# Attention and token-mixing MLP on one core: the fourth term of VectorE's exponential tiles by an accumulating DMA

## The chip, the cores and the metric

The kernel runs on one core of a Trainium2 chip. The metric is the device time of one execution in microseconds. The median of three runs of the kernel before is 754.1 us (753.49 to 754.58). All work is on one core: TensorE (PE) multiplies, ScalarE (ACT) and VectorE (DVE) compute elementwise, GpSimd (POOL) does little, SyncE (SP) issues the DMAs.

## What is computed

The input x has 2048 tokens of 640 features. It is normalised, goes through attention with 32 heads of 20 features, and is gated by a token-mixing MLP.

```python
xn = _layernorm(x, axis=-1)
# attention: 32 heads of 20
scores = einsum("bhqd,bhkd->bhqk", q, k) * (Dh ** -0.5)
p = softmax(scores, axis=-1)
o = einsum("bhqk,bhkd->bhqd", p, v)
s = o.reshape(B, S, D) @ wo
# MLP over the tokens, F = 1536
u = gelu(einsum("bsd,sf->bdf", layernorm(xn), w1) + b1)
g = silu(einsum("bdf,fs->bds", u, w2) + b2)
return x + s * g
```

What matters here is the softmax: 32 x 2048 x 2048 exponentials.

## The kernel before, in words

**Units and passes.** Scores are computed transposed: keys on the 128 partitions, queries along the free axis. A *unit* is one block of 128 keys by 512 queries of one head. Heads are taken in eight groups of four; a *pass* is one group with 512 queries, so 16 key blocks by 4 heads, 64 units. There are 2048 units in all. The four heads of a group are row-tiled on TensorE (32 rows each), so up to four score matmuls run side by side (`emit_st`, L1283). Values are column-tiled, four heads side by side (`emit_pv`, `pv_mm`, L1381), and accumulate in one PSUM bank.

**Two ways to the exponential.** ScalarE takes units in groups of two or three PSUM banks and writes exact exponentials as bf16 into `pt_sb` (`emit_exp`, L1313). VectorE takes *quads*, the four heads of one key block. For each head it adds a constant to the scaled score, clamps it at zero and rounds it to uint16 (`emit_op1`, L1324); the bits of this integer, read as bf16, are a piecewise linear approximation of the exponential. The result goes to buffer 0 of the quad in `dt_sb`, 128 x 4 x 512. To make the approximation better, the integer is shifted by the constants `DK = (0, 32, 64, 96)`: three more buffers of the quad get buffer 0 plus 32, 64 and 96 (`emit_top`, L1362, one instruction of 128 x 2048 each). The sum of the four, weighted by `AK`, is the exponential. The weights sit in the values: term 0 is multiplied with `v_sb`, terms 1 to 3 with scaled copies `vs_sb`. So a quad costs TensorE four value bursts, one for each term, where four units of ScalarE cost one.

**Who takes what.** Only the five key blocks in `RC` of each pass may become quads, since only for these are scaled values kept. `d_claimable` gives one out if a buffer is free, fewer than `NLIVE` quads are live and 16 units of the pass are left, else from the next pass. VectorE's units get a PSUM bank in two ways: the last bank of a three-bank group is lent to VectorE (`do_st`, if `dve_load` is below `LEND`), or the spare bank `JB` is used.

**Order of the work.** The order of the instructions on each engine is fixed when the program is built. The class `Prog` keeps a time for each engine; the main loop of `schedule` asks `pe_cands` and `eng_cands` what each engine could do next, takes what can start first by priority, and adds its planned cost. Hardware semaphores then hold each instruction until what it needs is done, but an engine never goes past its first waiting instruction. Besides scores and values, TensorE gets the projections, the MLP and the output product as *jobs* with priorities and due times (`add_job`, `add_bank_job`). `row_piece` puts single row-tiled steps of an MLP job beside scores that leave a row group free. `emit_fill` (L1398) adds zero products where TensorE would stand still. All DMAs are issued from SP on eight semaphore lanes (`Prog.dma`).

**Buffers.** `dt_sb` has `NTILE` = 8 buffers. A quad takes one at its first unit and one for each further term; a buffer comes free once the value product of its term is planned, buffer 0 once all terms are written and its own product is planned. `dquads` holds the quads whose values are due; only the first of the current pass is looked at.

Of the kernel before, what the change touches and what calls it, by code (L numbers as in the profile page):

```python
# [10 lines left out]
P = 128  # L11
# [28 lines left out]
class Prog:  # L40
# [3 lines left out]
    COMPUTE = ("pe", "act", "dve", "pool", "sp")  # L44
    LAT = {"pe": 55.0, "act": 55.0, "dve": 55.0, "pool": 80.0, "sp": 60.0}
    TAIL = {"pe": 170.0, "act": 118.0, "dve": 82.0, "pool": 60.0, "sp": 0.0}

    def __init__(self, nc, n_lanes=8):
        self.nc = nc
        self.n_lanes = n_lanes  # L50
        self.cengs = list(self.COMPUTE) + [f"d{i}" for i in range(n_lanes)]
# [8 lines left out]
        self.pipe = 0.0  # L60
        self.pe_end = 0.0
        self.low = 0
        self.lowt = 0.0
        self.alog = []
# [21 lines left out]
    def _add(self, eng, ceng, fn, reads, writes, name, extra_req=(), cost=100.0, tail=None):  # L86
# [50 lines left out]
        t.t0 = start  # L137
        if ceng not in self.COMPUTE:
            start = max(start, 700.0)
            if tail is not None:  # L140
                self.T[eng] = start + cost
                self.pipe = max(self.pipe, start) + cost
                t.fin = self.pipe - cost + tail
            else:
                self.T[eng] = start + 450.0
                self.pipe = max(self.pipe, start + 600.0) + cost
                t.fin = self.pipe + (1200.0 if self.pipe < 2500.0 else 2800.0 if cost > 800.0 else 1400.0)
        else:
            self.T[eng] = start + cost
            self.busy[eng] += cost  # L150
            t.fin = start + cost + (self.TAIL[eng] if tail is None else tail)
# [32 lines left out]
    def dma(self, fn, reads=(), writes=(), name="dma", lane=None, cost=3000.0, over=(), tail=None):  # L184
# [12 lines left out]
        return t  # L197

    def final_waits(self):
        for li in range(self.n_lanes):  # L200
# [10 lines left out]
    def emit(self, sems):  # L211
# [12 lines left out]
        def make(engname):  # L224
            def body(eng):
                for t in self.tasks[engname]:
# [5 lines left out]
                    ins = t.fn(eng)  # L232
                    if engname == "sp" and t.ceng.startswith("d"):
# [32 lines left out]
class _Kern:  # L266
# [9 lines left out]
    JB = 7  # L276
    RC = (0, 3, 6, 9, 12)
    NT = 2
# [6 lines left out]
    QK_LEAD = 6.0  # L285
    SLACK, MINJ = 0.0, 640.0
    ROOM = 6
    ROWM, ROWP, ROWN = 5, 2, 400
    lastrow = None
    MERGE = False  # L290
    OPM = 2
# [15 lines left out]
    SHARE = True  # L307
    VPRIO = 25.0
    QAT = (0.0, 0.0, 0.0, 0.0)
    ACTP = 30.0  # L310
    COLS = True
    NTILE, NLIVE, EARLY = 8, 3, True
    QC = ((0.5, 3.0), (3.2, 6.4), (9.0, 13.5), (14.0, 18.0), (19.0, 22.0))
# [4 lines left out]
    OPTS = (  # L318
        ("SLACK", (120.0, 40.0, 200.0, 320.0)),
        ("MINJ", (640.0, 320.0, 1000.0)),  # L320
        ("ROOM", (3, 6, 0)),
        ("DRIDE", (400.0, 150.0, 700.0)),
        ("LEND", (1800.0, 1300.0, 2400.0, 700.0, 0.0)),
        ("PARTS", ((2,), (2, 1), (3, 1), (1,), ())),
        ("LATE", (2.0, -9.0, 99.0)),
        ("DON", (True, False)),
        ("LONE", (False, True)),
        ("CONFL", (True, False)),
        ("TOPP", (38.0, 22.0)),
        ("EVP", (24.0, 36.0)),  # L330
        ("FGAP", (40.0, 150.0)),
        ("GROT", (1, 0)),
    )
    PLAN = ()
# [18 lines left out]
    def build(self):  # L353
# [4 lines left out]
        with es:  # L358
# [18 lines left out]
            sb("pt_sb", [P, self.RP, 512], bf)  # L377
            sb("dt_sb", [P, self.NTILE, 4, 512], u16)
            sb("zt_sb", [P, 2, 2, self.D], bf)
            sb("tr_sb", [P, 512], f32)  # L380
# [18 lines left out]
            for i in range(pr.n_lanes):  # L399
                sems[f"d{i}"] = E(nc.semaphore(f"sem_d{i}"))  # L400
            self.t = t
            self.schedule()
# [8 lines left out]
    def schedule(self):  # L411
# [716 lines left out]
        dquads = []  # L1128
        tfree = list(range(self.NTILE))
        dlive = [0]  # L1130
        dop1 = []
# [68 lines left out]
        def d_claimable():  # L1200
            if not self.DON:
                return None
            if tfree and dlive[0] < self.NLIVE:
                q0 = a_cur[0]
# [36 lines left out]
        def d_take(g, bk):  # L1241
            d = d_cur[0]
            if d is None:
                q, c, r = d_claimable()
                claimed.add((q, c))
                dlive[0] += 1
                d = d_cur[0] = dict(q=q, c=c, r=r, todo=[0, 1, 2, 3], tl=[tfree.pop(0), None, None, None], fin=[0.0] * 4, left=4, pk=0)
                stats["dve_units"] += 4
                nd_pass[q] += 1
# [70 lines left out]
        def emit_op1():  # L1320
# [12 lines left out]
            if d["left"] == 0:  # L1333
                dtop.append([d, 1])
                d["fin"][0] = tk.fin
                if self.EARLY:
                    dquads.append((0.0, d))

        def emit_top():
            d, k = dtop[0]  # L1340
# [26 lines left out]
            for j in range(k, k + n):  # L1367
                d["fin"][j] = tk.fin
            if k + n == 4:
                dtop.pop(0)  # L1370
                if not self.EARLY:
                    dquads.append((tk.fin, d))
                for j in range(2 if n == 2 else 1):
# [38 lines left out]
        def emit_pv(items, quads):  # L1412
# [4 lines left out]
            ends = [d for d, n_ in quads if d["pk"] + n_ == 4]  # L1417
            freed = []
            for d, n_ in quads:
                for k in range(d["pk"], d["pk"] + n_):  # L1420
                    for g in range(4):
                        seq.append(("d", d, k, g))
                    if k > (1 if self.MERGE else 0) or d["tl"][3] is not None:
                        freed.append(d["tl"][k])
                d["pk"] += n_
            items = sorted(items, key=lambda x: (x[3], x[1][2]))
            for x in items:
# [12 lines left out]
            for i, s in enumerate(seq):  # L1440
# [15 lines left out]
                else:  # L1456
# [8 lines left out]
                    avail.remove((fin, u, s0))  # L1465
            tfree.extend(freed)
            for d in ends:
                dlive[0] -= 1
                dquads[:] = [x for x in dquads if x[1] is not d]
# [83 lines left out]
        for w in (1, 0):  # L1553
# [3 lines left out]
        rw.append(("tag", "wr"))  # L1557
        add_job("wr", rw, ("xTd15",), 30.0)
        add_job("bload", [
            ("dma", small(lambda e: e.dma_start(bload_sb[:, 0:FC], B_b1.rearrange("(fc p) -> p fc", p=P))), [], [S_("bl1")],  # L1560
# [216 lines left out]
        def pe_cands(T):  # L1777
# [28 lines left out]
            if acc_ok[0] and pv_pass[0] < NP:  # L1806
# [5 lines left out]
                    f"v{half}_{y[0]}" in done and f"vs{G}_{r}" in done for y, r in zip(units[q][x[1]["c"]], x[1]["r"]))]  # L1812
                quads = quads[:1]
                pick, cnt = [], [0] * 4
# [20 lines left out]
                okp = bool(pick) and (min(cnt) >= 1 or len(pick) == rem or (tail and len(mine)))  # L1835
                if quads:
                    d0 = quads[0][1]
                    have = sum(f > 0.0 for f in d0["fin"])
                    left = have - d0["pk"]
                    whole = have == 4  # L1840
                    if left > 0 and whole:
                        if min(cnt) >= 1 or rem == len(pick):
                            pv.append(mk(pick, [(quads[0], left)]))
                            if len(pick) < rem or not pick:
                                pv.append(mk([], [(quads[0], left)]))
                        else:
                            pv.append(mk([], [(quads[0], left)]))
                    for n in self.PARTS:
                        if n < left or (n == left and not whole):
                            pv.append(mk([], [(quads[0], n)]))  # L1850
                if okp:
# [4 lines left out]
            for j in active:  # L1856
                s = j.steps[j.i]
                if s[0] == "pe":
                    late = late or now - j.at > self.LATE
                    n = 0  # L1860
                    for z in j.steps[j.i:]:
                        if z[0] == "row":
                            continue
                        if z[0] != "pe":
                            break
                        n += z[5]
                    jb.append((j.prio, pr.ready("pe", s[2], s[3]), lambda j=j: do_step(j, "pe"), s[5], n,
                               "pv" if len(s) > 6 else "full"))
            if ramp[0] or nomore_a():
                c = [x[:3] for x in ([sta] if sta else []) + ([std] if std else []) + pv + jb]  # L1870
# [74 lines left out]
        def dve_load(T):  # L1945
            x = max(0.0, pr.T["dve"] - T) + 602.0 * len(dop1)
            for d, k in dtop:
                x += (1730.0 if k == 1 else 1130.0) if self.MERGE else 600.0 * (4 - k)
            return x

        def row_piece(used):
# [48 lines left out]
        def do_st(grp, us):  # L2000
            T = pr.T["pe"]
            lend = None
            if (len(grp) >= self.LEND_MIN and len(us) == len(grp) and dveready[0] and (not ramp[0] or self.RLEND)
                    and dve_load(T) < self.LEND):
                lend = d_pick({u[2] for u in us[:-1]})
# [76 lines left out]
        def loads():  # L2082
# [8 lines left out]
            for x in {id(x): x for x in live}.values():  # L2091
                pe += 216.0 * (4 - x["pk"])
                d += (1730.0 if x["fin"][1] == 0.0 else 1130.0 if x["fin"][3] == 0.0 else 0.0) if self.MERGE else (
                    597.0 * sum(f == 0.0 for f in x["fin"][1:]))
            return a - done_cost["act"], pe - done_cost["pe"], d - done_cost["dve"]
# [5 lines left out]
        while True:  # L2101
# [17 lines left out]
            if (nomore or (a_cur[0] == NP - 1 and a_left(NP - 1) < self.D_GUARD)) and d_cur[0] is None and not dop1:  # L2119
                if not bankq and JB not in busybanks and JB not in bank_off:  # L2120
                    bank_off.add(JB)
# [15 lines left out]
            if bt is None:  # L2137
                break
            r, e = bt
# [46 lines left out]
```

## Time and profile before

| What | Value | How to read it |
|---|---|---|
| median of three runs | 754.1 us | 753.49 to 754.58 |
| profiled execution | 754.1 us | its own time |
| span of its profile | 752.3 us | first to last instruction; 1.8 us lie around it |
| granted TensorE clock | 0.999 | mean over the span |
| value products of quads, L1381 | 1536 + 512 matmuls | terms 1 to 3 with `vs_sb`, term 0 with `v_sb` |
| value products of ScalarE's units | 1616 matmuls | from `pt_sb` |
| score matmuls, L1283 | 2128, 376 ns mean | up to four side by side |
| GpSimd, 60 to 730 us | 0.6 us busy | one memset |
| DMA | 42.66 MB, mean 57 GB/s | all from SP, bursts for the MLP's weights |

Columns of a group line are: line, engine, operation, output<-input, shapes, count, then busy us, mean ns of one, and the engine's idle time just before them with what ended it. A matmul's end is modelled and neighbours overlap, so TensorE's busy time isn't TensorE at its peak; distances from start to start tell more.

### The profile page before, as it was taken

How to read it: one execution, taken by the hardware profiler on the slowest of the kernel's cores; microseconds unless marked ns; L12 is line 12 of the kernel's file. 1: busy time of each engine (PE TensorE's matmuls, PEld its weight loads, DVE VectorE, ACT ScalarE, POOL GpSimd, SP SyncE). 2: the span in 40 equal slices, each digit the busy share in tenths (PEclk: the TensorE clock that was granted, in tenths of full speed). 3: DMA queues.
4: the chain of work that ended last, by engine and by line, in shares of the span. 5: the costliest groups of instructions: out<-in, count | busy, mean ns of one | idle time of the engine just before them, and what ended most of it. 6: DMA issues, size and time to landing. Idle time of an engine off the chain costs nothing.

```text
span 752.3 us, 23672 instructions
## 1 busy us (share of the span) xinstructions
PE 716.3 (95%) x10561; PEld 243.6 (32%) x10561; DVE 719.0 (96%) x1320; ACT 730.0 (97%) x707; POOL 15.3 (2%) x23
## 2 busy tenths in 40 slices
PE   9899999999999999999999999999999999999997
PEld 7332222222233232323223332323233332333233
DVE  7889999999999999999999999999999999999996
ACT  5989999999999999999999999999999999999995
POOL 4200000000000000000000000000000000000000
PEclk9999999999999999999999999999999999999999
DMA  8754111110121031212111131301325501041102
GB/s 237 155 110 48 56 38 37 20 38 5 38 62 20 13 76 31 72 24 69 20 38 21 30 87 24 74 13 29 79 76 81 128 28 51 7 152 47 47 15 70
DMA packets 119738, 42.66 MB, mean 57 GB/s; under 512 B 79172, under 2 KB 118468, under 8 KB 119588
## 3 DMA queue, kind: packets, MB, share of 16 engines
q1 hardware_dynamic: 119636, 41.15, 23.4%
q8 instruction: 82, 1.34, 0.8%
q14 instruction: 20, 0.16, 0.1%
HBM read 26.37 MB, written 10.22 MB: 49 GB/s over the span
## 4 chain that ended last, share of the span: by engine, by line
ACT 76%; PE 18%; DVE 6%; issue 0%; DVEq 0%
ACT pt_sb L1313 74%; PE ps_all L1381 5%; PE ps_all L1283 5%; PE ps_all L648 5%; DVE dt_sb L1324 1%; PE ps_all L1408 1%; ACT zt_sb L849 1%; DVE dt_sb L1362 1%; ACT zt_sb L844 1%; DVE bst_sb L532 1%; DVE bst_sb L530 1%; DVE regC L548 1%; PE ps_all L965 1%; PE ps_all L633 0%; DVE v_sb L1114 0%; PE ps_all L746 0%
## 5 line engine op out<-in xcount | busy, mean ns | idle before, releaser
L1313 ACT ACTIVATE pt_sb<-ps_all 128x1024 bf16<-128x1024 f32 (+1 forms) x681 | 711.2, 1242 | 4.9 <-PE ps_all L1283 2.1
L1324 DVE TENSOR_SCALAR dt_sb<-ps_all 128x512 uint16<-128x512 f32 x496 | 328.4, 683 | 15.9 <-PE ps_all L1283 8.9
L1283 PE MATMUL ps_all<-qk_sb 32*128 32x512 bf16 (+1 forms) x2128 | 269.1, 376 | 26.4 <-ACT pt_sb L1313 22.9
L1362 DVE TENSOR_SCALAR dt_sb<-dt_sb 128x2048 uint16<-128x2048 uint16 x372 | 241.2, 689 | 1.5
L1283 PEld LDWEIGHTS ps_all<-qk_sb 32*128 32x128 bf16 x2128 | 68.4, 91 | 280.9 <-ACT pt_sb L1313 226.4
L1381 PE MATMUL ps_all<-dt_sb,vs_sb 128*21 128x512 bf16 (+1 forms) x1536 | 130.7, 376 | 0.9 <-DVE dt_sb L1362 0.5
L1381 PE MATMUL ps_all<-pt_sb,v_sb 128*21 128x512 bf16 (+1 forms) x1616 | 127.0, 374 | 1.9 <-DVE v_sb L1114 0.9
L648 PE MATMUL ps_all<-regC,regA 128*32 128x128 bf16 (+1 forms) x1472 | 65.5, 297 | 0.0
L648 PE MATMUL ps_all<-regB,regA 128*32 128x128 bf16 (+1 forms) x1480 | 65.2, 298 | 0.3 <-DVE qs_sb L698 0.3
L1381 PEld LDWEIGHTS ps_all<-dt_sb,vs_sb 128*21 128x21 bf16 x1536 | 33.4, 90 | 51.7 <-issue 31.2
L1381 PE MATMUL ps_all<-dt_sb,v_sb 128*21 128x512 bf16 (+1 forms) x512 | 49.2, 377 | 0.1
L1381 PEld LDWEIGHTS ps_all<-pt_sb,v_sb 128*21 128x21 bf16 x1616 | 30.9, 90 | 49.2 <-issue 35.9
L648 PE MATMUL ps_all<-xnT_sb,wqk_sb 128*32 128x512 bf16 x640 | 46.1, 382 | 0.0
L648 PEld LDWEIGHTS ps_all<-regB,regA 128*32 128x32 bf16 x1480 | 27.4, 96 | 23.3 <-issue 10.9
L648 PEld LDWEIGHTS ps_all<-regC,regA 128*32 128x32 bf16 x1472 | 27.8, 96 | 22.0 <-issue 10.6
L965 PE MATMUL ps_all<-wv_sb,xnT_sb 128*128 128x512 bf16 (+1 forms) x160 | 27.3, 301 | 0.0
L656 PE MATMUL ps_all<-regC,regA 32*128 32x512 bf16 x64 | 24.6, 384 | 0.0
L648 PE MATMUL ps_all<-wv_sb,xnT_sb 128*32 128x480 bf16 x320 | 22.1, 369 | 0.3 <-DVE qs_sb L1117 0.3
L1505 DVE STREAM_TRANSPOSE tr_sb<-ps_all 128x512 f32<-128x512 f32 x31 | 22.0, 711 | 0.0
L656 PE MATMUL ps_all<-regB,regA 32*128 32x512 bf16 x56 | 21.5, 384 | 0.0
L1381 PEld LDWEIGHTS ps_all<-dt_sb,v_sb 128*21 128x21 bf16 x512 | 13.0, 90 | 20.6 <-issue 14.2
L1398 PE MATMUL ps_all<-wp_sb,zw_sb 128*21 128x512 bf16 (+1 forms) x244 | 19.4, 373 | 0.0
(88 smaller groups left out, 348.5 us busy)
## 6 DMA issues: line engine op xcount, KB each, us to landing
regA<-in_B_w_dram SPq DMA_DIRECT2D x6, 1024.0 KB
regA<-in_B_w_dram SPq DMA_DIRECT2D x8, 768.0 KB
qk_sb<-qk_scratch_dram SPq DMA_DIRECT2D x56, 80.0 KB
qk_scratch_dram<-qs_sb SPq DMA_DIRECT2D x32, 128.0 KB
regA<-in_A_x_dram SPq DMA_DIRECT2D x6, 640.0 KB
ok_scratch_dram<-on_sb SPq DMA_DIRECT2D x96, 20.0 KB
out_dram<-regC SPq DMA_DIRECT2D x3, 640.0 KB
wqk_sb<-in_A_wqkv_dram SPq DMA_DIRECT2D x2, 480.0 KB
```

Of the source, the lines that this page charges most:

```text
L530: steps.append(("dve", lambda e, b=b: e.bn_stats(bst_sb[:, b, 0:6], regA[:, b, 0:320]), [sx], [s0], f"{nm}s0", 393.0))
L532: steps.append(("dve", lambda e, b=b: e.bn_stats(bst_sb[:, b, 6:12], regA[:, b, 320:640]), [sx], [s1], f"{nm}s1", 393.0))
L648: fns.append(lambda e, c=c, e_=e_: e.matmul(oc(c, e_), lhsT[:, c:e_], rhs, start=start, stop=stop, tile_position=(0, c)))
L656: row = lambda g: (lambda e: e.matmul(oc(0, 128), lhsT[32 * g:32 * g + 32, :], rhs[32 * g:32 * g + 32, :], start=False, stop=False, tile_p ...
L965: steps.append(("pe", lambda e, c=c: e.matmul(ap, oT_sb[:, c, b * 128:(b + 1) * 128], wo_ap[:, c, c0:c0 + n], start=(opens and c == 0), st ...
L1283: t = pr.pe(lambda e, outp=outp, lhsT=lhsT, rhs=rhs, g=g: e.matmul(outp, lhsT, rhs, start=True, stop=True, tile_position=(32 * g, 0)), rea ...
L1313: tk = pr.act(lambda e: e.activation(outp, inp, AF.Exp, scale=math.log(2.0) / 128.0), reads=[bank_slot[b] for b in banks[:n]], writes=[S_( ...
L1324: tk = pr.dve(lambda e: e.tensor_scalar(w, src, WOFF, 0.0, ALU.add, ALU.max), reads=[bank_slot[bk]], writes=[S_(f"dt{d['tl'][0]}_{g}")], n ...
L1362: tk = pr.dve(lambda e: e.tensor_scalar(dst, src, dk, None, ALU.add), reads=[S_(f"dt{b}_{g}") for b in inb for g in range(4)], writes=[S_( ...
L1381: pr.pe(lambda e: e.matmul(outp, lhsT, rhs, start=(k == 0), stop=last, tile_position=(0, 32 * g)), reads=reads, writes=[bank_slot[AB]], na ...
L1398: pr.pe(lambda e, outp=outp, rhs=rhs, g=g: e.matmul(outp, zw_sb[:, 0:DH + 1], rhs, start=False, stop=False, tile_position=(0, 32 * g)), re ...
L1505: steps.append(("dve", lambda e: e.transpose(tr_sb[:, :], ps(AB)), [bank_slot[AB]], [S_("tr")], f"epT{q}", 632.0))
```

## The change

For most quads the third L1362 (the fourth term, plus 96) is replaced by one DMA. A new tile `kc_sb`, 128 x 4 x 512 of uint16, is filled once with 96 by GpSimd. Once the value product of term 0 is planned, `emit_x` issues from GpSimd a DMA that adds `kc_sb` to buffer 0 in place, 512 KB; buffer 0 then holds the fourth term. So such a quad needs three buffers, not four. `x_ok` says which quads qualify: the planned queue of these transfers is at most 4 us behind VectorE's planned time, and the quad's pass isn't ScalarE's current one or has at least 16 units left. Other quads do the fourth term on VectorE as before.

The planner gets four lanes for these transfers and three costs: 950 ns on GpSimd to issue, 2900 ns to move, 2700 ns to land. The list of quads whose values are due may go past quads that lack only their fourth term. `dve_load` and the planned loads count the work left out. Besides:

- `NTILE` 8 to 7 (one buffer's room goes to `kc_sb`), `NLIVE` 3 to 4
- `RC` from (0, 3, 6, 9, 12) to (2, 5, 8, 11, 14)
- `SLACK` 0 to 80: scores for ScalarE may be planned 80 ns later than its need
- `ROWP` 2 to 1; `row_rest` now finishes row-tiled steps that are left over, at the end of a job or when nothing else can run
- `VPRIO` 25 to 24.5, `ACTP` 30 to 22
- the bank `JB` is given to the tail only once all MLP products are planned

`OPTS`, `LENDH`, `LEND1`, `JLATE` and `DLAG` change nothing as they stand: `PLAN` is empty in both, and the limits aren't reached.

```diff
+    NXL = 4
+    XISSUE, XMOVE, XTAIL = 950.0, 2900.0, 2700.0
...
+        if eng == "pool" and ceng != "pool":
+            self.T[eng] = start + self.XISSUE
+            self.xpipe = max(self.xpipe, start + self.XISSUE) + self.XMOVE
+            t.fin = self.xpipe + self.XTAIL
...
-    RC = (0, 3, 6, 9, 12)
+    RC = (2, 5, 8, 11, 14)
...
-    SLACK, MINJ = 0.0, 640.0
+    SLACK, MINJ = 80.0, 640.0
...
-    NTILE, NLIVE, EARLY = 8, 3, True
+    NTILE, NLIVE, EARLY = 7, 4, True
+    XLEFT, XQ = 16, 4000.0
...
+        def x_ok(d):
+            if "kc" not in done or pr.xpipe > pr.T["dve"] + self.XQ:
+                return False
+            return d["q"] > a_cur[0] or a_left(d["q"]) >= self.XLEFT
+
+        def emit_x(d):
+            b0 = d["tl"][0]
+            dst = dt_sb[:, b0, :, :]
+            sl_ = [S_(f"dt{b0}_{g}") for g in range(4)]
+            t = pr.xdma(lambda e: e.dma_start(dst, kc_sb[:, :, :], accum_op=ALU.add), [S_("kc")] + sl_, sl_,
+                        f"dX{d['q']}_{d['c']}")
+            d["tl"][3] = b0
+            d["fin"][3] = t.fin
...
-            if k + n == 4:
+            if k == 2 and not self.MERGE and x_ok(d):
+                d["x"] = True
                 dtop.pop(0)
...
+                if d["pk"] >= 1:
+                    emit_x(d)
+            elif k + n == 4:
+                dtop.pop(0)
...
+                if d["x"] and d["pk"] < 4 and d["tl"][3] is None:
+                    xs.append(d)
...
             tfree.extend(freed)
+            for d in xs:
+                emit_x(d)
...
+        add_job("kc", [("pool", lambda e: e.memset(kc_sb[:, :, :], int(self.DK[3])), [], [S_("kc")], "kc", 1800.0), ("tag", "kc")],
+                ("lnp14",), 43.0)
...
-                quads = quads[:1]
+                k = 0
+                while k < len(quads) - 1 and quads[k][1]["x"] and quads[k][1]["pk"] == 3:
+                    k += 1
+                quads = quads[:k + 1]
```

More of the change, by code (lines that the diff above doesn't have):

```diff
@@ L50, in __init__ @@
         self.n_lanes = n_lanes
-        self.cengs = list(self.COMPUTE) + [f"d{i}" for i in range(n_lanes)]
+        self.cengs = list(self.COMPUTE) + [f"d{i}" for i in range(n_lanes)] + [f"x{i}" for i in range(self.NXL)]
         self.cidx_of = {c: i for i, c in enumerate(self.cengs)}
@@ L60, in __init__ @@
         self.pipe = 0.0
+        self.xpipe = 0.0
+        self.xn = 0
         self.pe_end = 0.0
@@ L137, in _add @@
         t.t0 = start
-        if ceng not in self.COMPUTE:
+        if eng == "pool" and ceng != "pool":
+            self.T[eng] = start + self.XISSUE
+            self.xpipe = max(self.xpipe, start + self.XISSUE) + self.XMOVE
+            t.fin = self.xpipe + self.XTAIL
+        elif ceng not in self.COMPUTE:
             start = max(start, 700.0)
@@ L197, in dma, with xdma @@
         return t
+    def xdma(self, fn, reads, writes, name):
+        ceng = f"x{self.xn % self.NXL}"
+        self.xn += 1
+        t = self._add("pool", ceng, fn, reads, writes, name, extra_req=self.ctasks[ceng][-1:])
+        t.need_inc = True
+        return t
     def final_waits(self):
@@ L232, in body @@
                     ins = t.fn(eng)
-                    if engname == "sp" and t.ceng.startswith("d"):
+                    if t.ceng not in self.COMPUTE:
                         ins.then_inc(sems[t.ceng], 16)
@@ L285 @@
     QK_LEAD = 6.0
-    SLACK, MINJ = 0.0, 640.0
+    SLACK, MINJ = 80.0, 640.0
     ROOM = 6
-    ROWM, ROWP, ROWN = 5, 2, 400
+    ROWM, ROWP, ROWN = 5, 1, 400
     lastrow = None
+    LENDH, LEND1, JLATE = 0.0, 9999.0, 0.0
     MERGE = False
@@ L307 @@
     SHARE = True
-    VPRIO = 25.0
+    VPRIO = 24.5
     QAT = (0.0, 0.0, 0.0, 0.0)
-    ACTP = 30.0
+    ACTP = 22.0
     COLS = True
-    NTILE, NLIVE, EARLY = 8, 3, True
+    NTILE, NLIVE, EARLY = 7, 4, True
+    DLAG = 99.0
+    XLEFT, XQ = 16, 4000.0
     QC = ((0.5, 3.0), (3.2, 6.4), (9.0, 13.5), (14.0, 18.0), (19.0, 22.0))
@@ L318 @@
     OPTS = (
-        ("SLACK", (120.0, 40.0, 200.0, 320.0)),
+        ("SLACK", (0.0, 120.0, 40.0, 200.0, 320.0)),
         ("MINJ", (640.0, 320.0, 1000.0)),
-        ("ROOM", (3, 6, 0)),
+        ("ROOM", (6, 3, 0)),
         ("DRIDE", (400.0, 150.0, 700.0)),
         ("LEND", (1800.0, 1300.0, 2400.0, 700.0, 0.0)),
-        ("PARTS", ((2,), (2, 1), (3, 1), (1,), ())),
-        ("LATE", (2.0, -9.0, 99.0)),
+        ("PARTS", ((3, 1), (2,), (2, 1), (1,), ())),
+        ("LATE", (1.0, 2.0, -9.0, 99.0)),
         ("DON", (True, False)),
@@ L329 @@
         ("TOPP", (38.0, 22.0)),
-        ("EVP", (24.0, 36.0)),
-        ("FGAP", (40.0, 150.0)),
+        ("EVP", (36.0, 24.0)),
+        ("FGAP", (0.0, 40.0, 150.0)),
         ("GROT", (1, 0)),
+        ("JOBF", (4, 0, 8)),
     )
@@ L378, in build @@
             sb("dt_sb", [P, self.NTILE, 4, 512], u16)
+            sb("kc_sb", [P, 4, 512], u16)
             sb("zt_sb", [P, 2, 2, self.D], bf)
@@ L400, in build @@
                 sems[f"d{i}"] = E(nc.semaphore(f"sem_d{i}"))
+            for i in range(pr.NXL):
+                sems[f"x{i}"] = E(nc.semaphore(f"sem_x{i}"))
             self.t = t
@@ L1129, in schedule @@
         tfree = list(range(self.NTILE))
+        kc_sb = t["kc_sb"]
         dlive = [0]
@@ L1202, in d_claimable @@
                 return None
+            if bankq and not ramp[0] and nclaim[0] / UP - bankq[0].at > self.DLAG:
+                return None
             if tfree and dlive[0] < self.NLIVE:
@@ L1246, in d_take @@
                 dlive[0] += 1
-                d = d_cur[0] = dict(q=q, c=c, r=r, todo=[0, 1, 2, 3], tl=[tfree.pop(0), None, None, None], fin=[0.0] * 4, left=4, pk=0)
+                d = d_cur[0] = dict(q=q, c=c, r=r, todo=[0, 1, 2, 3], tl=[tfree.pop(0), None, None, None], fin=[0.0] * 4, left=4, pk=0, x=None)
                 stats["dve_units"] += 4
@@ L1337, in emit_op1 @@
                     dquads.append((0.0, d))
+        def x_ok(d):
[10 more added lines that the diff above has]
+            d["fin"][3] = t.fin
+            stats["x"] = stats.get("x", 0) + 1
         def emit_top():
@@ L1368, in emit_top @@
                 d["fin"][j] = tk.fin
-            if k + n == 4:
+            if k == 2 and not self.MERGE and x_ok(d):
+                d["x"] = True
                 dtop.pop(0)
-                if not self.EARLY:
-                    dquads.append((tk.fin, d))
+                if d["pk"] >= 1:
+                    emit_x(d)
+            elif k + n == 4:
+                dtop.pop(0)
                 for j in range(2 if n == 2 else 1):
@@ L1417, in emit_pv @@
             ends = [d for d, n_ in quads if d["pk"] + n_ == 4]
-            freed = []
+            freed, xs = [], []
             for d, n_ in quads:
@@ L1835, in pe_cands @@
                 okp = bool(pick) and (min(cnt) >= 1 or len(pick) == rem or (tail and len(mine)))
-                if quads:
-                    d0 = quads[0][1]
-                    have = sum(f > 0.0 for f in d0["fin"])
+                for qd in quads:
+                    d0 = qd[1]
+                    have = next((i for i, f in enumerate(d0["fin"]) if f == 0.0), 4)
                     left = have - d0["pk"]
@@ L1842, in pe_cands @@
                         if min(cnt) >= 1 or rem == len(pick):
-                            pv.append(mk(pick, [(quads[0], left)]))
+                            pv.append(mk(pick, [(qd, left)]))
                             if len(pick) < rem or not pick:
-                                pv.append(mk([], [(quads[0], left)]))
+                                pv.append(mk([], [(qd, left)]))
                         else:
-                            pv.append(mk([], [(quads[0], left)]))
+                            pv.append(mk([], [(qd, left)]))
+                    elif left > 0 and d0["x"] and left not in self.PARTS:
+                        pv.append(mk([], [(qd, left)]))
                     for n in self.PARTS:
                         if n < left or (n == left and not whole):
-                            pv.append(mk([], [(quads[0], n)]))
+                            pv.append(mk([], [(qd, n)]))
                 if okp:
@@ L1868, in pe_cands @@
                                "pv" if len(s) > 6 else "full"))
+                elif s[0] == "row" and nclaim[0] == NALL:
+                    x = j.rowstep[j.i]
+                    jb.append((j.prio, pr.ready("pe", x[2], x[3]), lambda j=j: row_rest(j), 320.0, 320.0, "st"))
             if ramp[0] or nomore_a():
@@ L1947, in dve_load, with row_rest, lend_ok @@
             for d, k in dtop:
-                x += (1730.0 if k == 1 else 1130.0) if self.MERGE else 600.0 * (4 - k)
+                x += (1730.0 if k == 1 else 1130.0) if self.MERGE else 600.0 * ((3 if x_ok(d) else 4) - k)
             return x
+        def row_rest(j):
+            x = j.rowstep[j.i]
+            for g in sorted(j.rows[j.i]):
+                self.lastrow = pr.pe(x[7](g), reads=x[2], writes=x[3], name=x[4] + "r", cost=pe_cost("st", 320.0), w=53.0,
+                                     after=self.lastrow)
+            j.rows[j.i].clear()
+            settle(j)
+        def lend_ok(T):
+            if max(0.0, pr.T["dve"] - T) + 602.0 * len(dop1) >= self.LEND1:
+                return False
+            x = dve_load(T)
+            if x < self.LEND:
+                return True
+            if x >= self.LENDH or not bankq:
+                return False
+            return nclaim[0] / UP - bankq[0].at < self.JLATE
         def row_piece(used):
@@ L2003, in do_st @@
             if (len(grp) >= self.LEND_MIN and len(us) == len(grp) and dveready[0] and (not ramp[0] or self.RLEND)
-                    and dve_load(T) < self.LEND):
+                    and lend_ok(T)):
                 lend = d_pick({u[2] for u in us[:-1]})
@@ L2093, in loads @@
                 d += (1730.0 if x["fin"][1] == 0.0 else 1130.0 if x["fin"][3] == 0.0 else 0.0) if self.MERGE else (
-                    597.0 * sum(f == 0.0 for f in x["fin"][1:]))
+                    597.0 * sum(f == 0.0 for f in x["fin"][1:3 if x["x"] else 4]))
             return a - done_cost["act"], pe - done_cost["pe"], d - done_cost["dve"]
@@ L2119, in schedule @@
             if (nomore or (a_cur[0] == NP - 1 and a_left(NP - 1) < self.D_GUARD)) and d_cur[0] is None and not dop1:
-                if not bankq and JB not in busybanks and JB not in bank_off:
+                if not bankq and JB not in busybanks and JB not in bank_off and all(x in done for x in m2pe):
                     bank_off.add(JB)
@@ L2137, in schedule @@
             if bt is None:
-                break
+                j = next((j for j in active if j.steps[j.i][0] == "row"), None)
+                if j is None:
+                    break
+                row_rest(j)
+                continue
             r, e = bt
```

## The prediction

> **What bounds the kernel now.** I read the page's busy times first, then one stretch of the table by stage (40 us, after the ramp, to 740 us, before the tail), then the groups by form, the waits, and last a few lines of the timeline. Columns of the stage line: start:end, length, then busy us and instruction count of PE, PEld, DVE, ACT and POOL.
>
> ```profile
> PE 716.3 (95%) x10561; PEld 243.6 (32%) x10561; DVE 719.0 (96%) x1320; ACT 730.0 (97%) x707; POOL 15.3 (2%) x23
> ...
> 40.00:740.00 700.00, 672.31 (x10090) 217.24 (x10090) 680.09 (x1188) 698.53 (x677) 0.63 (x1) 1.00 0.21 48
> ...
> ACT 76%; PE 18%; DVE 6%; issue 0%; DVEq 0%
> ```
>
> Between 40 and 740 us ScalarE is idle for 1.5 us of 700, VectorE for 20, TensorE for 28. The chain of waits is ScalarE's exponentials for three quarters. So ScalarE sets the end, VectorE is the second owner of the same work (the exponentials of 2048 score units), and TensorE, which serves both, is nearly full.
>
> ```profile
> L1313 ACT ACTIVATE pt_sb<-ps_all 128x1024 bf16<-128x1024 f32 x491 | 481.3, 1127 | 0.9 <-PE ps_all L1283 0.5
> L1324 DVE TENSOR_SCALAR dt_sb<-ps_all 128x512 uint16<-128x512 f32 x496 | 328.4, 683 | 15.9 <-PE ps_all L1283 8.9 <-PE ps_all L656 5.7
> L1313 ACT ACTIVATE pt_sb<-ps_all 128x1536 bf16<-128x1536 f32 x190 | 285.9, 1541 | 4.0 <-PE ps_all L1381 1.9 <-PE ps_all L1283 1.7
> L1362 DVE TENSOR_SCALAR dt_sb<-dt_sb 128x2048 uint16<-128x2048 uint16 x372 | 241.2, 689 | 1.5
> L1398 PE MATMUL ps_all<-wp_sb,zw_sb 128*21 128x512 bf16 x224 | 18.5, 382 | 0.0
> ```
>
> Here the reader sees the split: 496 units, 124 quads of four, are VectorE's, the other 1552 ScalarE's. A quad costs VectorE 4 x 328.4/496 + 3 x 241.2/372 = 2.65 + 1.94 = 4.59 us; everything else on VectorE is 719.0 - 328.4 - 241.2 = 149.4 us. A unit taken from ScalarE turns a 1536-wide exponential into a 1024-wide one: 1541 - 1127 = 414 ns, so 1.66 us a quad. L1398 is filler: 61 bursts of four with the 20 narrow ones, put where TensorE would stand still.
>
> ```profile
> 301.17 0.39 PE L1283 MATMUL ps_all<-qk_sb 32*128 32x512 bf16 x3
> ...
> 301.50 0.40 PE L1381 MATMUL ps_all<-dt_sb,v_sb 128*21 128x512 bf16 x4
> ...
> 301.72 0.39 PE L648 MATMUL ps_all<-regC,regA 128*32 128x512 bf16 x4
> ...
> 302.04 0.39 PE L1283 MATMUL ps_all<-qk_sb 32*128 32x512 bf16 x3
> ```
>
> Four column-tiled matmuls start 0.22 us before the next four (301.50 to 301.72); between row-tiled and column-tiled ones lie 0.32 or 0.33, so a switch costs 0.10 to 0.11. TensorE runs back to back here.
>
> **What the Trainium skill says.** "DMA: Bandwidth & Descriptors", section "SWDGE vs HWDGE vs iDMA": an accumulating DMA can only be issued from GpSimd, whose cores write its descriptors. Its section "Anatomy of one DMA" gives about 2.0 us plus bytes/436e3 us for one. "Collectives: The Full Stack", section "The bandwidth ceiling", says that an adding transfer reads two sources and so runs at half rate. The trace of before has no accumulating DMA and cannot confirm these. "SBUF — State Buffer", section "Who interferes with whom": GpSimd and a VectorE instruction that uses both ports exclude each other for a whole instruction. With this the trace agrees, in the one place of the middle where GpSimd works:
>
> ```profile
> 518.78 0.63 POOL L1669 MEMSET wqk_sb<- 128x640 bf16 x1 [485.07 <-PE ps_all L691]
> ...
> 518.94 1.62 DVE L1362 TENSOR_SCALAR dt_sb<-dt_sb 128x2048 uint16<-128x2048 uint16 x2
> ```
>
> Two L1362 take 1.29 us elsewhere (303.77 us); here 0.33 more.
>
> **The change, part by part, against the profiled execution: 754.1 us, of which the span is 752.3 and 1.8 lies around it; the median of the three runs is also 754.1.**
>
> *Removed.* One L1362 of each quad that qualifies. A quad qualifies if 16 units of its pass are still unclaimed when its third term is planned. Passes have 64 units, about 44 of them ScalarE's; from the claim to the third term is some 6 us, in which ScalarE takes some 13 units at 1552 in 700 us. Quads claimed with 16 to 29 left fail: about a fifth (estimate). Savings at 124 quads: 0.8 x 124 x 0.648 = 64.3 us of VectorE.
>
> *Moved over.* VectorE's free time takes quads from ScalarE until both end together. A quad costs 4.59 - 0.8 x 0.648 = 4.08 us on VectorE and frees 1.66 on ScalarE, so the end moves by 1.66/(1.66 + 4.08) = 0.289 of the savings: 18.6 us, with 18.6/1.66 = 11 quads moved, to 135. Five key blocks per pass are open to quads in both versions, which allows over 150.
>
> *What is late next: TensorE.* A quad has four value bursts of 0.216 instead of one: 11 x 0.648 = 7.1 us more, in a span 18.6 shorter: 25.7 us. It has 28 idle in the middle and about two thirds of the filler (61 x 0.216 = 13), so 37. From 5% of slack 1.5% would be left, and the order on TensorE is fixed, so gaps cannot all be used. I take off 5.5 us for this and for waits at the fourth term; the bounds are 0 (all gaps usable) and 18.6 (none).
>
> *Added: the transfers*, some 108 of 512 KB, from GpSimd. The planner allows 0.95 to issue, 2.9 to move, 2.7 to land, 6.55 us. By the skill's price, 2.0 + 524288/436e3 = 3.2 us, and 4.4 with two reads (estimate). Issue added, 5.4: the allowance holds if engines are free. They carry 23.4% of queue work on average; the transfers add 108 x 2.9 = 313 us, another 42%. Meeting a weight load of 1 MB, a transfer can be some 3 us late. TensorE then stands at the fourth term, and behind it queue the next scores, for which ScalarE waits after at most one exponential of 1.1 to 1.5 us. Hidden if late by under a microsecond, in full above.
>
> *Added: GpSimd against VectorE.* Bounds: nothing (descriptors written in short pieces, or beside L1324, which reads PSUM), and about 0.65 us per transfer (a whole L1362 blocked), 70 us. The transfer may go only after the third term's L1362. What follows it is mostly L1324:
>
> ```profile
> 309.16 1.90 DVE L1362 TENSOR_SCALAR dt_sb<-dt_sb 128x2048 uint16<-128x2048 uint16 x3
> 310.96 1.29 DVE L1324 TENSOR_SCALAR dt_sb<-ps_all 128x512 uint16<-128x512 f32 x2
> ```
>
> So I take 0.1 us per transfer, 11 us of VectorE, 11 x 0.289 = 3.2 us of the end.
>
> *GpSimd's queue.* Each transfer waits for VectorE's third term and TensorE's first product; behind it are only later transfers, the L1669 memset and the tail's one addition, neither near its due time. SP's queue is passed by nothing.
>
> *The rest, at nothing.* The constant's memset: 2048/1280 x 1.16 us (L510's duration) = 1.9 us on GpSimd (estimate), in its gap of 2.37 us before L565; if it comes late, L565 and the scaling after it move by up to 1.9. The other key blocks for quads, one more quad allowed in pass 0, one buffer fewer with one more live quad: three buffers a quad instead of four pay for it; uncovered, a quad starts late and ScalarE keeps its units, 1.66 us each. SLACK 80 lets scores come 0.08 us late: 0 to 681 x 0.08 x 1/10 = 5 us (estimate), against some switches of 0.105 saved; I take zero.
>
> *Sum.* 18.6 - 5.5 - 3.2 = 9.9 us. Span 742.4, run **744.2 us**, against the equal median.
>
> **The rivals.**
> - *TensorE becomes the bound (15%).* For: 5% slack, 0.32 us a switch cycle, every extra quad costs it 0.648. If none of its gaps can be used, ScalarE keeps its share: 754.1 less some 2, 752 us. Against: filler shows usable gaps.
> - *Late transfers (25%), the slower side.* TensorE's in-order wait at the fourth term takes the place of the L1362. It decides from 9.9/108 = 0.09 us of mean stall per transfer. With one in ten late by 1.5 us past its cover: 108 x 0.15 = 16 us on 744.2, so 761. For: queue work in bursts, GpSimd shut out while L1362 runs, a plan with 0.06 us of margin. Against: 6.55 us allowed against 5.4 estimated.
> - *Few quads qualify (6%).* A third: 41 x 0.648 = 27 us of VectorE, x 0.289 = 7.7, half of it lost as above: 750.
>
> **How the numbers follow.** The main case has 54%, from 735 (nearly all of the 18.6) to 751. Below 736 I leave 8%, above 763 12%, so the range is 736 to 763; the main case's own is 736 to 751. About 0.2%, 1.5 us, is what a measurement of this kernel can tell from no change. Faster: 0.52 of the main case, 0.05 of the few, 0.10 of the TensorE case, 0.67. Slower: 0.25, and 0.02 from the others' edges, 0.27. Same: 0.06.
>
> **What would show it.** Right: L1362 at 2 per quad plus some 27, L1324 above 530, ScalarE still idle for only a few us between ramp and tail, TensorE above 97% busy there, less L1398. Wrong: weight loads of L1381 waiting on a DMA into dt_sb for more than 10 us in total (late transfers); L1362 well above 689 ns (GpSimd's hold); VectorE under 94% busy with as many L1324 as now (TensorE's bound); fewer than 60 transfers (few qualify).

## The result and the profile after

The changed kernel takes 772.57 us (median of four runs, 771.35 to 773.95) against 754.34 us before: a ratio of 1.0243, 95% interval 1.0219 to 1.0266. It is slower by 2.4%, where 1.3% faster was forecast. The profiled execution took 771.35 us, its span is 769.6.

Busy times of the page and the stage from 40 to 740 us, kernel after:

```profile
PE 712.8 (93%) x10517; PEld 240.9 (31%) x10517; DVE 693.9 (90%) x1271; ACT 724.2 (94%) x707; POOL 96.6 (13%) x109
...
40.00:740.00 700.00, 655.00 (x9739) 207.35 (x9736) 638.20 (x1113) 674.39 (x661) 78.78 (x85) 0.99 0.56 111
...
ACT 49%; PE 27%; DVE 9%; DMA 9%; SPq 4%; issue 1%; POOL 0%; DVEq 0%
```

All three engines have less work than before (ScalarE 724.2 for 730.0 us, VectorE 693.9 for 719.0), and all three wait more. ScalarE, idle for 1.5 us of this stretch before, is now idle for 25.6. In the chain of waits stand two owners that were not there: DMA with 9% and SP's queue with 4%.

The groups, kernel after, show what the exchange of work came to:

```profile
L1338 ACT ACTIVATE pt_sb<-ps_all 128x1024 bf16<-128x1024 f32 (+1 forms) x682 | 705.1, 1171 | 27.9 <-PE ps_all L678 14.3
L1349 DVE TENSOR_SCALAR dt_sb<-ps_all 128x512 uint16<-128x512 f32 x516 | 342.7, 681 | 42.6 <-PE ps_all L678 21.0
...
L1402 DVE TENSOR_SCALAR dt_sb<-dt_sb 128x2048 uint16<-128x2048 uint16 x302 | 198.8, 685 | 3.1 <-PE ps_all L1424 2.2
L1373 POOL DMA_DIRECT2D dt_sb<-kc_sb x85 | 79.3, 944 | 618.1 <-PE ps_all L1424 317.7
```

516 units are 129 quads, five more than before; 85 of them (66%) use a transfer, so there are 3 x 129 - 85 = 302 instructions of L1402 (the former L1362). Their mean is 685 ns, for 689 before.

The waits, kernel after (engine, line, what it waited for: us in total, times, longest):

```profile
PEld ps_all L1424 <- DMA dt_sb<-kc_sb: 11.7, 10, 3.5
...
PEld ps_all L670 <- DMA regA<-in_B_w_dram: 10.6, 1, 10.6
...
PE ps_all L1424 <- DMA dt_sb<-kc_sb: 8.8, 7, 3.2
```

TensorE waits on two kinds of DMA. (L1424 holds the value products, formerly L1381, and L670 the MLP's products, formerly L648.) A product's weight load (PEld) and its matmul (PE) wait for the same event, so the two rows of one cause must not be added. It is 11.7 us for transfers into `dt_sb`, in ten places, and 10.6 us in one place for weights of the MLP: 22.3 us that the kernel before has none of.

The largest wait on a transfer, in the timeline of the kernel after (start, length, engine):

```profile
211.08 0.40 SPq L805 DMA_DIRECT2D regA<-in_B_w_dram  x1
...
213.08 0.87 POOL L1373 DMA_DIRECT2D dt_sb<-kc_sb  x1 [3.16 <-PE ps_all L1424]
...
223.58 0.40 PE L1424 MATMUL ps_all<-dt_sb,vs_sb 128*21 128x512 bf16 x4 [3.23 <-DMA dt_sb<-kc_sb]
...
224.34 1.02 ACT L1338 ACTIVATE pt_sb<-ps_all 128x1024 bf16<-128x1024 f32 x1 [3.26 <-PE ps_all L1308]
```

A weight load of 1 MB goes out at 211 us, the transfer two microseconds later. Its product starts only at 223.58, 10.5 us after the issue, where the planner had counted 6.55. TensorE stands for 3.2 us, the scores behind the product are late, and ScalarE stands for 3.3: the in-order wait passes through in full. That the weight load is what made this transfer late is tested in e2.

The other kind, first in SP's queue, then on the engines, kernel after:

```profile
573.18 29.61 SPq L957 DMA_TRANSPOSE xnT_sb<-ok_scratch_dram  x16
602.84 1.49 SPq L972 DMA_DIRECT2D xnT_sb<-zw_sb  x1
604.42 5.05 SPq L812 DMA_DIRECT2D regA<-in_B_w_dram  x2
...
613.53 0.11 PEld L670 LDWEIGHTS ps_all<-regB,regA 128*32 128x32 bf16 x4 [10.60 <-DMA regA<-in_B_w_dram]
...
614.73 1.02 ACT L1338 ACTIVATE pt_sb<-ps_all 128x1024 bf16<-128x1024 f32 x1 [10.46 <-PE ps_all L678]
```

SP needs 29.61 us to issue the 16 transposing loads of the attention output, and two weight loads are queued behind them. In the kernel before the same 16 take 22.10:

```profile
567.11 22.10 SPq L935 DMA_TRANSPOSE xnT_sb<-ok_scratch_dram  x16
```

GpSimd's queue at the end of this stretch, kernel after:

```profile
598.00 1.88 POOL L1373 DMA_DIRECT2D dt_sb<-kc_sb  x2 [12.85 <-PE ps_all L1424]
601.71 0.87 POOL L1373 DMA_DIRECT2D dt_sb<-kc_sb  x1 [1.84 <-PE ps_all L1308]
```

These three transfers land 5.4 to 7.6 us after their issue, the last at 609.3, so the two weight loads meet them.

A long wait costs more than its length. After the 10.6 us three score matmuls side by side take 0.61 us, from 617 on 0.39 again (kernel after):

```profile
615.59 0.61 PE L1308 MATMUL ps_all<-qk_sb 32*128 32x512 bf16 x3
...
617.10 0.39 PE L1308 MATMUL ps_all<-qk_sb 32*128 32x512 bf16 x3
```

The granted TensorE clock in the trace is 0.50 of full speed from 609 to 615 us. Its mean is 0.54 from 606 to 617, and 0.57 from 224 to 228 and from 313 to 317, at the ends of the three longest waits (10.6, 3.5 and 2.6 us). In the kernel before it is 1.00 between 40 and 740 us. TensorE works at half clock for some 3.4, 3.2 and 3.6 us in these places, which loses up to 5 us (an estimate from the three lengths). That the waits bring the clock down is read from the order in time; no run tests it alone.

### The profile page after: what moved, and what is told of

Same layout as the page of the kernel before. It is cut to its first block, busy times and chain, and to the rows that moved or that the text cites. A ratio compares the mean times of both kernels' runs of the same rounds, so it can differ in the third digit from the quotient of the medians.

```text
span 769.6 us, 23685 instructions
## 1 busy us (share of the span) xinstructions
PE 712.8 (93%) x10517; PEld 240.9 (31%) x10517; DVE 693.9 (90%) x1271; ACT 724.2 (94%) x707; POOL 96.6 (13%) x109
## 4 chain that ended last, share of the span: by engine, by line
ACT 49%; PE 27%; DVE 9%; DMA 9%; SPq 4%; issue 1%; POOL 0%; DVEq 0%
ACT pt_sb L1338 48%; PE ps_all L1424 8%; PE ps_all L1308 8%; PE ps_all L670 7%; DMA dt_sb<-kc_sb 7%; SPq L957 4%; DVE dt_sb L1349 3%; DVE dt_sb L1402 2%; DMA regA<-in_B_w_dram 1%; PE ps_all L1451 1%; ACT zt_sb L871 1%; PE ps_all L655 1%; DVE regC L570 1%; PE ps_all L987 0%; DMA xnT_sb<-regC 0%
## 5 line engine op out<-in xcount | busy, mean ns | idle before, releaser
L1349 DVE TENSOR_SCALAR dt_sb<-ps_all 128x512 uint16<-128x512 f32 x516 | 342.7, 681 | 42.6 <-PE ps_all L678 21.0
L1402 DVE TENSOR_SCALAR dt_sb<-dt_sb 128x2048 uint16<-128x2048 uint16 x302 | 198.8, 685 | 3.1 <-PE ps_all L1424 2.2
L1373 POOL DMA_DIRECT2D dt_sb<-kc_sb x85 | 79.3, 944 | 618.1 <-PE ps_all L1424 317.7
L1424 PE MATMUL ps_all<-dt_sb,vs_sb 128*21 128x512 bf16 (+1 forms) x1596 | 138.1, 378 | 9.9 <-DMA dt_sb<-kc_sb 8.8
L1424 PE MATMUL ps_all<-pt_sb,v_sb 128*21 128x512 bf16 (+1 forms) x1596 | 123.2, 376 | 3.0 <-DVE v_sb L1136 2.1
L670 PE MATMUL ps_all<-regB,regA 128*32 128x128 bf16 (+1 forms) x1472 | 66.7, 298 | 10.1 <-DMA regA<-in_B_w_dram 10.1
L670 PE MATMUL ps_all<-regC,regA 128*32 128x512 bf16 (+1 forms) x1468 | 69.4, 299 | 1.0 <-issue 0.7
L1424 PEld LDWEIGHTS ps_all<-dt_sb,vs_sb 128*21 128x21 bf16 x1596 | 36.1, 90 | 65.3 <-issue 35.2
L1424 PE MATMUL ps_all<-dt_sb,v_sb 128*21 128x512 bf16 (+1 forms) x532 | 50.7, 377 | 0.8 <-DVE tr_sb L1544 0.2
L670 PE MATMUL ps_all<-xnT_sb,wqk_sb 128*32 128x512 bf16 x640 | 47.2, 384 | 0.0
L1424 PEld LDWEIGHTS ps_all<-pt_sb,v_sb 128*21 128x21 bf16 x1596 | 28.8, 90 | 44.9 <-issue 33.6
L670 PEld LDWEIGHTS ps_all<-regB,regA 128*32 128x32 bf16 x1472 | 27.5, 96 | 32.6 <-issue 10.6
L670 PEld LDWEIGHTS ps_all<-regC,regA 128*32 128x32 bf16 x1468 | 28.5, 96 | 24.6 <-issue 11.6
L678 PE MATMUL ps_all<-regB,regA 32*128 32x512 bf16 x64 | 25.0, 391 | 0.0
L670 PE MATMUL ps_all<-wv_sb,xnT_sb 128*32 128x480 bf16 x320 | 22.5, 369 | 0.1
L1424 PEld LDWEIGHTS ps_all<-dt_sb,v_sb 128*21 128x21 bf16 x532 | 13.3, 90 | 20.6 <-issue 13.1
```

Of the source, the lines that this page charges most:

```text
L670: fns.append(lambda e, c=c, e_=e_: e.matmul(oc(c, e_), lhsT[:, c:e_], rhs, start=start, stop=stop, tile_position=(0, c)))
L678: row = lambda g: (lambda e: e.matmul(oc(0, 128), lhsT[32 * g:32 * g + 32, :], rhs[32 * g:32 * g + 32, :], start=False, stop=False, tile_p ...
L1349: tk = pr.dve(lambda e: e.tensor_scalar(w, src, WOFF, 0.0, ALU.add, ALU.max), reads=[bank_slot[bk]], writes=[S_(f"dt{d['tl'][0]}_{g}")], n ...
L1373: t = pr.xdma(lambda e: e.dma_start(dst, kc_sb[:, :, :], accum_op=ALU.add), [S_("kc")] + sl_, sl_, f"dX{d['q']}_{d['c']}")
L1402: tk = pr.dve(lambda e: e.tensor_scalar(dst, src, dk, None, ALU.add), reads=[S_(f"dt{b}_{g}") for b in inb for g in range(4)], writes=[S_( ...
L1424: pr.pe(lambda e: e.matmul(outp, lhsT, rhs, start=(k == 0), stop=last, tile_position=(0, 32 * g)), reads=reads, writes=[bank_slot[AB]], na ...
```

## The experiments

**Theory A:** the new order of work is good as laid out, and the loss is the traffic of the transfers, which land late and make other loads late. **Rivals:** B, GpSimd's issue holds VectorE, or the new order itself is bad; C, transfers are late by themselves, whatever else runs; D, the rules and the lost buffer cost the time. The first two experiments keep the changed kernel's instructions and their order; only the size of a DMA differs.

**e1, small transfers.**

```diff
-t = pr.xdma(lambda e: e.dma_start(dst, kc_sb[:, :, :], accum_op=ALU.add), [S_("kc")] + sl_, sl_,
+t = pr.xdma(lambda e: e.dma_start(dst[:, 0, 0:128], kc_sb[:, 0, 0:128], accum_op=ALU.add), [S_("kc")] + sl_, sl_,
...
```

> Same instructions in the same order as the changed kernel, but each of the 85 transfers adds only to the first 128 of 2048 columns of a partition (32 KB in place of 512 KB); the rest of the fourth term is left out. Theory A (the order as laid out is good, and the loss is transfers that are late or make loads late): no wait of TensorE on a transfer, the 10 us wait for the MLP's weights gone or under 4 us, 746 to 752 us. Rival B (the loss is GpSimd's issue holding VectorE, or the new order itself): 765 us or more, since all issues and the whole order stay.

748.8 us; the ratio to before is 0.9938 (0.9916 to 0.9959): 0.6% faster than the kernel before, and inside theory A's range. The stage of e1, and its landing times:

```profile
40.00:740.00 700.00, 670.73 (x10123) 218.85 (x10134) 656.90 (x1153) 692.03 (x678) 80.42 (x87) 1.00 0.26 53
...
DMA to landing us min/median/max: 2.2/2.9/7.0
```

ScalarE's idle time falls from 25.6 to 8.0 us. TensorE's waits on transfers are 0.3 us, for weights 0.5. All 85 issues on GpSimd are still there, with a mean of 946 ns for 944, so theory B falls. The bytes of the transfers cost 772.57 - 748.8 = 23.8 us, near the 22.3 us of waits counted above. The stretches of half clock are gone between 40 and 740 us too, so e1 does not separate their share from that of the waits.

**e2, small weight loads.** The loads of the MLP's weights take `dst[:, 0:1, :]` of `src[:, 0:1, :]`, one sixteenth.

> Same order as the changed kernel, transfers whole, but each load of the MLP's weights moves one sixteenth of its bytes; the products run on what is left in the buffer. Theory A: the three long waits that met such a load (3.2, 2.3 and 10.1 us on TensorE) shrink to under half, 760 to 764 us; the waits near 382, 490 and 495 us that met other traffic stay. Rival C (transfers are late by themselves, whatever else runs): the waits on transfers stay near 20 us, only the 10 us wait shrinks, 764 to 768 us. Rival B: 770 or more.

758.79 us, 1.2 us under the range. TensorE's wait on transfers falls from 11.7 to 4.7 us. The waits at 223.6 and 313.6, 3.5 and 2.6 us long, are gone. So about 7 of the 11.7 us come from transfers that meet a weight load; what makes the rest late was not tried. The 20 us in the expectation counted both PEld and PE and should have been about 12; C's claim that these waits stay is wrong all the same. The weights still come 7.5 us late, although they are small: they stand behind the transposing loads, which take 28.48 us here. The whole gain, 772.57 - 758.79 = 13.8 us, is more than the 10.1 by which these waits shrink; the two shorter stretches of half clock are gone as well.

**e3, weights first.**

```diff
-add_job("oT", reload_steps(), qkall + v1all + epall, 40.0)
+add_job("oT", reload_steps(), qkall + v1all + epall + ("w2_7",), 40.0)
```

> The 16 transposing loads of the attention output (L957) are allowed only once the last weight load of the MLP has been issued, so no weight load stands behind them on SP's queue. Theory A: the 10 us wait for weights goes and nothing takes its place, 760 to 763 us; waits on transfers stay near 20 us. Rival B: the wait was hidden, 769 or more, or the output product waits for the later transposes at the end.

767.09 us (762.53 to 770.18), a miss. The wait for weights is gone, but in the profiled run, the slowest, the waits on transfers are 18.2 us in 13 places, for 11.7 in ten. A new one of about 3 us stands near 640 us, where the transposing loads now run (from 623.58, 30.49 us on SP). Moving the loads moved the collision. The fastest run lies inside theory A's range, so not every execution loses this.

**e9, twelve small transfers.** The changed kernel's order, but the transfers of quads in passes 23 to 26 move 32 KB.

> Order of the changed kernel; of the 85 transfers only the 12 of passes 23 to 26, which fall around the 16 transposing loads, add to 128 of 2048 columns (the rest of their fourth term is left out), the other 73 stay whole. Theory A (a handful of transfers slow the transposing loads, which hold SP's queue and so the weights): the transposing loads take about 22 us in place of 29.6, the wait for weights falls from 10 to under 3 us, the waits on transfers at 224 and 314 us stay, 762 to 765 us. Rival (the weights are late through the new order alone): the wait stays near 10 us, 770 or more.

762.13 us. SP's queue in e9:

```profile
575.81 22.99 SPq L957 DMA_TRANSPOSE xnT_sb<-ok_scratch_dram  x16
598.85 0.76 SPq L972 DMA_DIRECT2D xnT_sb<-zw_sb  x1
599.70 1.43 SPq L812 DMA_DIRECT2D regA<-in_B_w_dram  x2
```

The transposing loads are back at 22.99 us, and the wait for weights falls from 10.6 to 0.2 us, while the waits on transfers stay (11.8). These twelve transfers cost 772.57 - 762.13 = 10.4 us, by slowing SP's queue and not by landing late themselves. SP's queue is slower in two places: the transposing loads by 29.61 - 22.99 = 6.6 us, and the issue of the two weight loads themselves by 5.05 - 1.43 = 3.6.

**e5 and e6, half the bytes, and a copy that doesn't add.** e5 transfers `dst[:, 0:2, :]`, e6 leaves out `accum_op`.

> Order of the changed kernel, each transfer adds to two of the four heads' parts (256 KB in place of 512); the other half of the fourth term is left out. Theory A (engine time of the transfers): landing between the 2.9 us of 32 KB and the 5.9 of 512 KB, about 4.4, and a time between 748.8 and 772.6, nearer the lower end since the order allows 6.55 us: 750 to 757. If the loss went with the number of transfers and not their bytes: over 762.

> Order of the changed kernel, each transfer of 512 KB copies the constant into the buffer and doesn't add: one read in place of two (the fourth term's exponentials are left out). Theory A1 (the second read is what fills the engines): landing about 4.4 us, engine share of the GpSimd queue about half of 31.8%, 750 to 757 us, like half the bytes. Theory A2 (the written bytes count, not the reads): landing near 5.9 us and 765 to 773 us.

753.52 us (748.75 to 759.63) and 754.4 us (750.68 to 759.21), both within their ranges; the intervals of their ratios to before include 1 (0.9964 to 1.0022, and 0.9986 to 1.0034). The twelve runs of e5 spread over 10.9 us, the 23 of the kernel before beside them over 1.5. The spread goes with the granted clock, 0.987 in the longest run and 0.999 in the shortest, so one trace doesn't stand for all executions of e5. The software queue's line of each page (packets, MB, share of 16 engines), first the changed kernel's:

```profile
q0 software_dynamic: 12240, 44.57, 31.8%
```

then e5's:

```profile
q0 software_dynamic: 12240, 22.29, 17.6%
```

then e6's:

```profile
q0 software_dynamic: 12240, 44.57, 16.1%
```

An adding transfer of 512 KB takes 0.318 x 769.6 / 85 = 2.88 us of all 16 engines. A plain copy of the same bytes takes 0.161 x 752.3 / 85 = 1.42 us, half, and costs as little as half the adding bytes. Median landing is 5.9, 4.0 and 4.3 us. The Trainium skill ("Collectives: The Full Stack", section "The bandwidth ceiling") gives a factor of about two for ReduceScatter, whose add needs two reads, against AllGather, which copies; for these transfers within SBUF it is 2.0.

**e4 and e7, the rules alone.** `x_ok` returns False in both; e7 also has `NTILE` back at 8, with the constant's tile cut to a strip.

> The changed kernel with no quad allowed to use a transfer: all other edits (7 buffers, 4 live quads, other key blocks, SLACK 80, priorities) stay, every fourth term is VectorE's. Theory A: the rules are not what costs, 752 to 760 us, no ScalarE gap over 1 us. Rival D (the rules or the lost buffer cost): 765 us or more.

> No transfers, and the eighth buffer back (the constant's tile cut to a strip); all other edits of the rules stay. If the 8 us that the rules alone lose come from the lost buffer, 752 to 757 us; if they come from the other rules, 758 to 764.

762.07 us for e4, 2 us above the expectation, and 760.58 us for e7. Neither has a DMA wait of the kind above. The edits beside the transfer, with no transfer, cost 8.0 us and with the buffer back 6.6, so the buffer isn't the main part. In the traces ScalarE is busy for 734.7 us in e4, for 730.0 before, and VectorE takes 488 units, for 496; between 40 and 740 us ScalarE is idle for 5.9 us, for 1.5. Which of the other edits does it was not tried: each of them reorders everything. Theory D holds for this part, not for the 18 us.

**e8 and e10, two versions meant to beat both.** Both issue the weight loads first and plan a transfer later:

```diff
-t.fin = self.xpipe + self.XTAIL
+t.fin = self.xpipe + self.XTAIL + min(self.XSHARE * max(0.0, self.pipe - start), 5000.0)
```

with XSHARE 1 and XTAIL 3800 in e8. e10 has XTAIL 4300 and no transfers in the first five passes. Each also has other planner settings (SLACK, and in e8 ROWP and priorities, among them).

> A version meant to beat both: weight loads ahead of the transposing loads, a transfer planned to land 1.1 us later than in the changed kernel and later still by what SP's queue has planned at its issue, and other rules. Theory A: waits on transfers under 5 us, no wait for weights, 748 to 754 us. If lateness can't be planned for (waits still near 15 us): 758 or more.

> Second version meant to beat both: weight loads first, no transfers in the first five passes, transfers planned to land 1.6 us later than in the changed kernel and later by what SP's queue has planned, other rules. Theory A: 73 transfers, waits on them under 3 us, none for weights or qs_sb, 747 to 753 us, under the kernel before. If 756 or more, the traffic costs in other places than these waits.

e8: 765.57 us, a miss. The waits on transfers are down to 3.4 us, but a new wait stands early on. Timeline of e8:

```profile
74.51 0.69 DVE L1137 CAST qs_sb<-ps_all 128x512 bf16<-128x512 f32 x1 [6.94 <-DMA qk_scratch_dram<-qs_sb]
75.26 0.14 PEld L671 LDWEIGHTS ps_all<-xnT_sb,wqk_sb 128*32 128x32 bf16 x8 [6.73 <-DVE qs_sb L1137]
...
76.89 1.45 ACT L1339 ACTIVATE pt_sb<-ps_all 128x1536 bf16<-128x1536 f32 x1 [6.68 <-PE ps_all L1309]
```

The store that frees `qs_sb` came late; VectorE waited for it, TensorE for VectorE, ScalarE for TensorE. In SP's queue four copies stand ahead of the stores, first e8, with three transfers issued between 53.8 and 61.3 us, then the kernel before:

```profile
59.00 8.75 SPq L1592 DMA_DIRECT2D qk_sb<-qk_sb  x4
```

```profile
55.47 3.26 SPq L1544 DMA_DIRECT2D qk_sb<-qk_sb  x4
```

That the transfers are what slows them is an inference; e8 was not run with small ones.

e10: 757.08 us (753.51 to 760.53), ratio 1.0039 (1.0023 to 1.0055), a miss too. Waits on transfers are 4.1 us, ScalarE's idle time between 40 and 740 us is 5.8. The spread over its 14 runs goes broadly with the clock again, and its trace is of one of the shorter ones, 754.93, so it doesn't show where the other runs lose. It is the best with whole transfers, 15.5 us under the changed kernel, and still behind the kernel before. No version here beats that with the whole sum computed.

## Why the prediction was wrong, point by point

- **The step that failed** is "I take off 5.5 us for this and for waits at the fourth term". It priced TensorE's gaps and the waits in one term, with bounds of 0 and 18.6; the bytes of the transfers alone cost 23.8 us (e1), with 22.3 us of DMA waits in the trace.
- Half of that was foreseen. The rival of late transfers named the in-order wait, a bound of 0.09 us of mean stall and 0.15 as its own case; measured are 11.7/85 = 0.14. (Its 761 adds up to 760.) Its 3 us for a transfer that meets a weight load is near the 3.5 and 2.6 of the two longest waits. It was put second, because 5.4 us of estimated landing was held against an allowance of 6.55. The median, 5.9, indeed fits. But 33 of the 85 take longer than 6.55, up to 10.6, and the longest waits come from collisions with the weight loads (e2).
- The other half wasn't foreseen, and one sentence shut it out: "SP's queue is passed by nothing." Nothing is passed in the order, but SP's loads are slowed by the transfers. Slower transposing loads hold SP's queue, and the weight loads behind them start late and are themselves issued more slowly: 10.4 us from twelve transfers (e9).
- "The rest, at nothing" was wrong by 8.0 us (e4). The bounds given for SLACK and the buffers, 0 to 5 us, were too narrow for edits that reorder the whole program.
- The gain was of the right kind. With the same rules, leaving the fourth term to transfers of 32 KB brings 762.07 - 748.8 = 13.3 us, for 18.6 in the sum; VectorE takes 129 quads in e1, for 122 in e4, and ScalarE's busy time falls from 734.7 to 722.1 us. A smaller share qualified (66% for 80%); the 44 ScalarE units a pass in that estimate should have been 1552/32 = 48.5. And "until both end together" didn't come: VectorE is idle for 43 us between 40 and 740 in e1, for 20 before, so the plan didn't turn all of the freed time into quads.
- The sum by the runs: rules +8.0, freed VectorE -13.3, traffic +23.8, together +18.5; before, in the same series, is 754.1. (The three are differences between neighbours in one chain of runs, so they add up whatever the causes.) That e1, without the traffic, comes within 5 us of the 744.2 forecast is partly luck: -13.3 + 8.0 stands there for the -18.6 + 5.5 + 3.2 of the prediction.
- TensorE as the bound, the rival with 15%, didn't come: it is 93% busy, and in e1, at 95%, it carries the new order with ScalarE at 97%.
- GpSimd against VectorE, priced at 3.2 us, didn't show on VectorE: the 45 L1402 that run for at least 0.2 us beside an issue on GpSimd take 690 ns on average, the 251 with none beside them 684. It shows on the other side, kernel after:

```profile
207.06 1.18 POOL L1373 DMA_DIRECT2D dt_sb<-kc_sb  x1 [16.45 <-PE ps_all L1424]
207.32 2.03 DVE L1402 TENSOR_SCALAR dt_sb<-dt_sb 128x2048 uint16<-128x2048 uint16 x3
209.05 0.87 POOL L1373 DMA_DIRECT2D dt_sb<-kc_sb  x1 [0.81 <-DVE dt_sb L1402]
```

The issue that lies beside L1402 takes 1.18 us, the next, which meets only its last 0.3 us, 0.87. Over the trace the 19 issues with 0.7 us or more of L1402 beside them take 1.10 us on average, the 49 with none 0.88. So of the mutual exclusion that the prediction took from the Trainium skill ("SBUF — State Buffer", section "Who interferes with whom"), these issues show a longer issue on GpSimd and next to nothing on VectorE; that the shared ports are the reason is not tested.

## What to carry to other kernels

Work moved from a full engine to DMA engines that are mostly idle isn't free when another queue uses them in bursts: price it by what those transfers do to the loads that other engines wait for in order, and to the issue time of a queue that has more behind it. Read a transfer's landing time by its maximum, not its median, if a statically ordered engine waits for it. The cheapest test is to keep the order and shrink only the bytes: it splits traffic from order in one run. And look at the granted clock after a long wait, since the wait's own length may not be its whole cost.

## What was not expected of the hardware

An adding DMA of 512 KB within SBUF takes 2.0 times the engine time of a plain copy (2.88 for 1.42 us). It is also dearer to issue on GpSimd: 944 ns on average for 634, 869 for 537 in the shortest; the averages contain what GpSimd loses beside L1402. The 32 KB transfer still takes 2.9 us to land, so about half of the 5.9 us doesn't go with the bytes. SP's issue of 16 transposing loads stretches from 22.1 to 29.6 us under this traffic.
